# A transformer block on one core: the gated-shift copies rebuilt in one tensor, and the query/key weights loaded by head halves

## The chip, the cores and the metric

The kernel runs on one core of one Trainium2 chip. The metric is the device time of one execution in microseconds. Ten runs of the kernel before stand beside one profiled execution.

## The reference, cut to what matters

One sequence of 2048 rows with 448 features goes through attention over 8 dilated keys (16 heads of 28), and then through an MLP block whose first half shifts quarters of its features along the sequence:

```python
def _A_ref(x, wqkv, wo):                 # attention
    q, k, v = split(x @ wqkv)            # 16 heads of 28
    idx = pos[:, None] - 2 * arange(8)   # keys at 0, 2, ... 14 rows back
    attn = softmax(where(idx >= 0, q . k[idx] * scale, -1e9))
    return (attn . v[idx]) @ wo

def _B_ref(x, w1, w2, w3, w4):
    h = _gelu(_layernorm(x) @ w1)
    c = D // 4                           # 112
    g0 = h[:, :, 0*c:1*c] moved down one row      (zero row in front)
    g1 = h[:, :, 1*c:2*c] moved up one row        (zero row at the end)
    g2 = h[:, :, 2*c:3*c] moved down two rows
    g3 = h[:, :, 3*c:   ] moved up two rows
    hs = concatenate([g0, g1, g2, g3]) @ w2
    x1 = x + hs
    return x1 + _gelu(_layernorm(x1) @ w3) @ w4

h = x + _A_ref(_layernorm(x), wqkv, wo)
return h + _B_ref(_layernorm(h), w1, w2, w3, w4)
```

## The kernel before, in words

The sequence is cut into four chunks of 512 rows (c = 0 to 3). Inside a chunk, even and odd rows are kept apart as two parities p, so a shift by two rows is a shift by one column, and a shift by one row swaps the parities. All tensors are bf16 with sums in f32.

For each chunk the kernel normalises the rows and transposes them (phase_A1, L623; chunks 0 and 1 on TensorE, chunks 2 and 3 by transposing DMAs), projects values (phase_V, L654) and queries and keys (phase_QK, L700), forms scores, exponentials and weighted values (phase_att, L716: operations S, E and AV), divides by the sums (through a DMA to memory and back for chunks 2 and 3), projects with wo (phase_WO, L804), and enters the MLP: normalise and transpose by DMA, matmul with w1, gelu (phase_B1, L816). The second matmul with w2 (phase_B2, L877) and the large pair w3 and w4 (phase_W3, L900, phase_B3, L934) run over groups of tiles that lag the chunks (GROUPS, L871), since the shifts reach into the next chunk.

*Names.* Operations carry tags: V_c, QK_c.0 and QK_c.2 with evictions QK_c.e0 to e3, S_c.g, E_c.g, AV_c.g for head half g, WO_c, W1_c, W2_g, W3_g, W4_g. A PE operation V, QK, WO, W1, W2 or W3 is four passes of 64-row tiles that use both halves of the array at once (quad, L414); S uses 28-row tiles, AV 32-column tiles, W4 and the PE transposes the whole array.

*Order.* Nothing is scheduled at run time. Each operation is recorded once with its dependencies, and the table _ORDER (L235) writes out one global order by operation number, with a letter where the engine was open ("a" ACT, "v" DVE, "p" GpSimd) and the PSUM banks after the colon; schedule (L159) reads it, and _emit_plan (L194) adds the semaphore waits that the order doesn't already imply. Each engine then runs its part in order. All instructions are issued by one line (L1407), so the profile's line is the same everywhere and groups are told apart by tensor names. SP issues almost all DMAs; a DMA that has to wait for its data holds up those behind it on SP. START (L232; used at L1394 to L1400) sets at which instruction offset modulo 256 an engine's code starts. WARM (L229, L478) is the number of matmuls on zeros that TensorE runs while the first loads are under way.

*Loads at the start.* The four tiles of chunk 0 come first (L459, L460), on SP and ACT in turn; then wqk in two pieces of 448 KB and wv in two of 224 KB on SP (win_load, L449; each piece holds two of four row windows k of the weights); then chunks 1 to 3 of x. Query and key weights are then padded from 28 to 32 columns a head by four copies, one for each row window w (pad_wqk, L646 to L652), on ACT and DVE. QK needs all four.

*The shifted gelu.* W1_c yields two PSUM tiles. The first becomes gA with one gelu (L838). The second, three planes of 256 columns, becomes gtm with one gelu (L842). Then twelve copies put it, shifted, into gB (four copies of 32 rows and two planes, L844 to L847) and gC (eight of 32 or 16 rows and one plane, L848 to L852), each with its own offset for each group of rows; in the last chunk three DVE memsets clear edge columns (L853, L854). Each copy is on ACT or DVE, as _ORDER says (shift, L370). g_rows (L856) gives the matmul W2 its rows of gA, gB and gC. w1_p holds w1 with its columns permuted to match (L528 to L534), and w2_s its rows (L519 to L526).

## Time and profile before

| | us |
|---|---|
| median of 10 runs | 192.98 |
| lowest, highest | 192.15, 194.65 |
| profiled execution, its own time | 192.86 |
| its span | 191.1 |
| PE busy | 182.9 |
| DVE busy | 128.8 |
| ACT busy | 112.2 |
| GpSimd (POOL) busy | 41.8 |

The span runs from the first to the last instruction of the profiled execution; 1.76 us of its time lie around it. Busy times are sums over instructions; PE is matmul time, and loading of weights (PEld) lies beside it. In the timeline a row gives start, length, engine, operation, output and input tensor, their shape and a count; in brackets is the idle time before it and what ended it. "issue" there means that the engine waited for nothing that the profile shows. A name such as arena is shared: it holds the attention weights first and the large gelu later. w_p is w1_p, w_s is w2_s or a weight of the large pair, ps is PSUM.

### The profile page before, as it was taken

Reading aid. Unit: us, or ns where it says so; the run is one execution under the profiler, and the core shown is the slowest. Engines: PE = TensorE matmul, PEld = TensorE weight load, DVE = VectorE, ACT = ScalarE, POOL = GpSimd, SP = SyncE. Lnnn points to the kernel's source line nnn. Section 1 sums busy time; section 2 is a strip of 40 time slices with the busy share of each in tenths; the row PEclk is TensorE's granted clock in tenths of the full one; section 3 lists DMA queues with packets and bytes.
Section 4 is the critical chain, followed back from the end, with each engine's and each line's share of the span. In section 5 each row is a group of like instructions: output and inputs, shape, how many; then the busy total and the mean of one; then the engine's idle time right before and its main releaser. Section 6 shows DMA issues by size and latency. Waiting matters only on the chain.

```text
span 191.1 us, 6790 instructions
## 1 busy us (share of the span) xinstructions
PE 182.9 (96%) x2999; PEld 102.6 (54%) x2999; DVE 128.8 (67%) x313; ACT 112.2 (59%) x149; POOL 41.8 (22%) x101
## 2 busy tenths in 40 slices
PE   7899999998897998999999999999999999999994
PEld 2455556554555573577556464444566568454551
DVE  7799998999985789999773379894038970001241
ACT  2869899598859849938658930117691326554000
POOL 4137500607104503006900002043000320000000
PEclk9999999999999999999999999999999999999999
DMA  5965317325499765620641800507000233000021
GB/s 145 342 212 158 83 32 145 37 33 109 135 141 227 199 166 130 78 81 3 121 109 55 199 3 1 139 20 173 10 0 27 47 97 100 3 0 3 3 99 51
DMA packets 32479, 17.77 MB, mean 93 GB/s; under 512 B 22524, under 2 KB 31932, under 8 KB 32444
## 3 DMA queue, kind: packets, MB, share of 16 engines
q1 hardware_dynamic: 32156, 17.05, 38.5%
q8 instruction: 25, 0.41, 0.9%
q10 hardware_dynamic: 288, 0.23, 0.4%
q14 instruction: 10, 0.08, 0.1%
HBM read 10.07 MB, written 1.90 MB: 63 GB/s over the span
## 4 chain that ended last, share of the span: by engine, by line
PE 73%; ACT 10%; DVE 10%; DMA 4%; issue 1%
PE ps L1407 73%; DMA actT<-lntm 3%; ACT qk L1407 2%; ACT pt L1407 2%; DVE st L1407 2%; ACT gC L1407 2%; DVE rzb L1407 2%; DMA xin<-in_A_x_dram 1%; DVE osb L1407 1%; DVE xin L1407 1%; DVE oT L1407 1%; ACT gtm L1407 1%; ACT lntm L1407 1%; ACT arena L1407 1%; DVE lntm L1407 1%
## 5 line engine op out<-in xcount | busy, mean ns | idle before, releaser
L1407 PE MATMUL ps<-actT,w_s 64*128 64x512 bf16 (+2 forms) x560 | 44.2, 312 | 0.0
L1407 PE MATMUL ps<-w_s,arena 128*128 128x448 bf16 x224 | 43.4, 353 | 0.1
L1407 DVE TENSOR_TENSOR xb<-ps,xb 128x448 bf16<-128x448 f32 (+1 forms) x26 | 18.4, 724 | 32.8 <-PE ps L1407 32.7
L1407 ACT ACTIVATE arena<-ps 128x512 bf16<-128x512 f32 (+2 forms) x40 | 29.0, 767 | 16.9 <-PE ps L1407 16.6
L1407 PEld LDWEIGHTS ps<-actT,w_s 64*128 64x128 bf16 x560 | 26.4, 94 | 16.9 <-DVE xb L1407 0.4
L1407 PEld LDWEIGHTS ps<-w_s,arena 128*128 128x128 bf16 x224 | 21.4, 98 | 20.9 <-issue 0.6
L1407 PE MATMUL ps<-hT,arena 64*128 64x512 bf16 x224 | 25.9, 377 | 0.2
L1407 POOL TENSOR_TENSOR rstd<-vtmp,mhalf 128x4 f32<-128x4 f32 (+1 forms) x16 | 18.5, 1154 | 1.1
L1407 DVE BATCH_NORM_STATS2 st<-xin 128x6 f32<-128x448 bf16 x32 | 18.1, 606 | 0.1
L1407 ACT ACTIVATE pt<-ps 128x1024 bf16<-128x1024 f32 x16 | 15.7, 1022 | 3.3 <-PE ps L1407 3.2
L1407 PEld LDWEIGHTS ps<-hT,arena 64*128 64x128 bf16 x224 | 10.7, 94 | 12.0 <-ACT qk L1407 0.7
L1407 ACT ACTIVATE lntm<-xin,nmr,rstd 128x512 bf16<-128x512 bf16 x13 | 10.2, 808 | 9.0 <-POOL nmr L1407 8.5
L1407 POOL TENSOR_SCALAR vtmp<-mv 128x4 f32<-128x4 f32 (+1 forms) x16 | 4.6, 287 | 49.9 <-DVE mv L1407 49.0
L1407 PE MATMUL ps<-arena,hT 64*64 64x448 bf16 (+1 forms) x248 | 15.1, 352 | 0.3 <-DVE hT L1407 0.3
L1407 ACT ACTIVATE qk<-ps 128x1024 bf16<-128x1024 f32 x14 | 13.9, 1021 | 2.3 <-PE ps L1407 2.2
L1407 PE MATMUL ps<-wo_s,oT 64*128 64x448 bf16 x128 | 13.1, 350 | 0.6 <-ACT vt L1407 0.5
L1407 PE MATMUL ps<-actT,w_p 64*128 64x512 bf16 (+1 forms) x140 | 13.0, 333 | 0.2 <-DMA actT<-lntm 0.2
L1407 POOL TENSOR_SCALAR nmr<-mv 128x4 f32<-128x4 f32 (+1 forms) x16 | 3.9, 246 | 42.0 <-DVE mv L1407 41.8
L1407 ACT ACTIVATE lntm<-xb,nmr,rstd 128x512 bf16<-128x512 bf16 x5 | 4.0, 811 | 15.1 <-POOL nmr L1407 15.1
L1407 DVE COPY gC<-gtm 32x256 bf16<-32x256 bf16 (+1 forms) x15 | 3.4, 227 | 13.3 <-ACT gtm L1407 12.9
L1407 DVE TENSOR_TENSOR pt<-pt,msk 128x1024 bf16<-128x1024 bf16 x16 | 10.5, 682 | 0.6 <-ACT pt L1407 0.5
L1407 PEld LDWEIGHTS ps<-arena,hT 64*64 64x64 bf16 (+1 forms) x248 | 7.6, 107 | 5.7 <-DVE hT L1407 0.5
(90 smaller groups left out, 226.9 us busy)
## 6 DMA issues: line engine op xcount, KB each, us to landing
w_s<-in_B_w_dram SPq DMA_DIRECT2D x6, 448.0 KB, 4.9
rzb<-rz_scratch SPq DMA_DIRECT2D x8, 256.0 KB, 4.4
out_dram<-xb SPq DMA_DIRECT2D x16, 112.0 KB, 2.1
xin<-in_A_x_dram SPq DMA_DIRECT2D x3, 448.0 KB, 7.3
arena<-in_A_wqkv_dram SPq DMA_DIRECT2D x2, 448.0 KB, 5.8
w_s<-in_B_w_dram SPq DMA_DIRECT2D x2, 336.0 KB, 4.8
arena<-in_A_wqkv_dram SPq DMA_DIRECT2D x2, 224.0 KB, 5.1
w_s<-in_B_w_dram SPq DMA_DIRECT2D x2, 224.0 KB, 2.8
```

The source lines that it names most:

```text
L1407: inst = getattr(eng, meth)(**kw)
```

## The change

1. gB, gC and gtm become one tensor gBC with four planes. The second gelu writes planes 0 to 2 of the chunk's columns directly. Seven copies then work inside gBC: two move 32 rows of planes 0 and 1 left by one or two columns, one copies plane 2 of all 128 rows to plane 3, and four write shifted pieces of plane 2 over parts of plane 3, after that one. In the last chunk some of them are one or two columns longer, and the three memsets are gone. Edge clears and g_rows follow.
2. Columns of w1_p and the 16-row pieces of w2_s are permuted to match; their number is the same.
3. wv is loaded ahead of wqk in the program, and wqk comes in eight pieces of 128 x 2 x 224 elements (448-byte rows): by head half h, window pair k, and query or key e; pieces with e above h are on ACT's queue. The four pad copies go by (h, k), so that QK_0.0 needs two of them, and QK_0.2 the other two.
4. Costs that the order was planned with change (bw, occ, lat); these are not instructions.
5. WARM is 13 instead of 14, START 132 instead of 128, and _ORDER is written anew: 843 operations instead of 861. It moves work on every engine. The largest moves: the clear of wo_s and the masks' clears stand before the first statistics on DVE; the first exp table load follows the first transposed copies on ACT; both evictions QK_3.e2 and QK_3.e3 are on DVE; AV_2.0 and AV_2.1 both stand before W1_0; S_3.0 stands before W2_1 and W3_0 after WO_2; on SP the last transposing DMA of chunk 3 stands after the transposing DMA of chunk 0's MLP input and a load of w4; GpSimd's w1_p copies come later. PE issues 2998 matmuls instead of 2999, and changes its kind of tiling 48 times instead of 51.

```diff
@@ -226,47 +226,46 @@
         op.clock = oc
     return plan
 
-WARM = 14
+WARM = 13
 LATE = 2
 
-START = 128
+START = 132 
 _ORDER = """
-2 1 4 3 7 6 8 5 12 17 0 16 13 15 45 65 74 64 67 68 79 21 19 18:7 22 20 28 23 24 25 26 29 27 35 30 32 36:7 33:6
...
+18 2 71 80 0 23 21 20 22 85 84 19 70 88 73 24:7 1 3 8 68 69 4 65 11 10 9 27 74 25 28 32 26 29 34 30 33 35 36 31
...
 """.split() 
@@ -304,9 +303,7 @@
     zz = oT[:, 0, :]
     rzb = sb("rzb", [128, 4, 512], F32)
     gA = sb("gA", [128, 2, 2, HALF + 2], BF16)
-    gB = sb("gB", [128, 2, HALF + 4], BF16)
-    gC = sb("gC", [128, HALF + 4], BF16)
-    gtm = sb("gtm", [128, 2, 768], BF16)
+    gBC = sb("gBC", [128, 4, HALF + 4], BF16)
     xin = sb("xin", [128, NTL, D], BF16)
     xb = sb("xb", [128, NTL, D], BF16)
     lntm = sb("lntm", [128, 3, 4, 2, 256], BF16)
@@ -376,6 +373,8 @@
         if not on_pool:
             del op.opts["pool"]
         op.occ = {e: v - {"dve": 82, "pool": 20, "act": 93}[e] for e, v in op.lat.items()}
+        if not on_pool:
+            op.occ = {e: v + {"dve": 0, "act": 25, "pool": 0}[e] for e, v in op.lat.items()}
         return op
 
     def pool(meth, lat, **kw):
@@ -446,20 +445,26 @@
     def xt(t, c, il, n):
         return t[:, 4 * c:4 * c + 4, :].rearrange("p (a u) d -> p a u d", a=2) if n == 4 else t[:, 4 * c + il, :]
 
-    def win_load(name, dst, src, nbytes, engs):
+    def win_load(name, dst, src, nbytes, engs, bw=290.0):
 
         for k in range(2):
             dma("%s%d" % (name, k), dst[:, 2 * k:2 * k + 2, :],
                 src[192 * k:192 * k + 256, :].rearrange("(c k) n -> k c n", k=128), nbytes / 2, engs[k],
-                430.0)
+                430.0, bw)
 
     tag("init0")
     dve("memset", 320, ap=zz[:], constant=0.0)
     tag("load0")
     for il in range(4):
-        dma("x0_%d" % il, xt(xin, 0, il, 1), x_rows(A_x, 0, il, 1), 128 * D * 2, ("sp", "act")[il % 2])
-    win_load("wqk", wqk_s, A_wqkv[:, 0:2 * D], 512 * 2 * D * 2, ("sp", "sp"))
-    win_load("wv", wv_s, A_wqkv[:, 2 * D:3 * D], 512 * D * 2, ("sp", "sp"))
+        dma("x0_%d" % il, xt(xin, 0, il, 1), x_rows(A_x, 0, il, 1), 128 * D * 2, ("sp", "act")[il % 2], bw=450.0)
+    win_load("wv", wv_s, A_wqkv[:, 2 * D:3 * D], 512 * D * 2, ("sp", "sp"), 190.0)
+    for h in range(2):
+        for k in range(2):
+            for e in range(2):
+                o = D * e + D // 2 * h
+                dma("wqk%d%d%d" % (h, k, e), wqk_s[:, 2 * k:2 * k + 2, o:o + D // 2],
+                    A_wqkv[192 * k:192 * k + 256, o:o + D // 2].rearrange("(c k) n -> k c n", k=128), 128 * D * 2,
+                    "act" if e > h else "sp", 430.0, 280.0)
     tag("load1")
     for c in range(1, NCH):
         dma("x%d" % c, xt(xin, c, 0, 4), x_rows(A_x, c, 0, 4), 128 * 4 * D * 2)
@@ -506,9 +511,8 @@
         dve("memset", 480, ap=w1_p[:, :, 384:640], constant=0.0)
         pool("memset", 140, ap=gA[:, :, :, 0:1], constant=0.0)
         pool("memset", 140, ap=gA[:, :, :, HALF + 1:HALF + 2], constant=0.0)
-        pool("memset", 140, ap=gB[:, :, 0:2], constant=0.0)
-        pool("memset", 140, ap=gB[:, :, HALF:HALF + 2], constant=0.0)
-        pool("memset", 140, ap=gC[:, 0:2], constant=0.0)
+        pool("memset", 140, ap=gBC[:, :, 0:2], constant=0.0)
+        pool("memset", 140, ap=gBC[:, :, HALF + 2:HALF + 4], constant=0.0)
 
     def load_attn_out():
         tag("load2")
@@ -522,15 +526,14 @@
             128 * D * 2)
         for g in range(4):
             for h in range(2):
-                k = 64 * h + 32 * (g // 2) + 16 * (1 - g % 2)
+                k = ((32, 0, 48, 16), (64, 112, 80, 96))[h][g]
                 dma("w2%d" % (3 + 2 * g + h), w2_s[k:k + 16, 3, :], w2v[96:112, g, :], 16 * D * 2)
         w1v = w1_s[:].rearrange("k w (g d) -> k w g d", d=G)
         tag("w1p")
         shift(w1_p[:, :, 0:256].rearrange("k w (g d) -> k w g d", d=64), w1v[:, :, :, 0:64], 1024, True)
         shift(w1_p[:, :, 256:384].rearrange("k w (g d) -> k w g d", d=32), w1v[:, :, :, 64:96], 512, True)
         for x in range(2):
-            for g, o in ((x, 384), (2 + x, 480), (2 + x, 544), (x, 576)):
-                o += 16 * (1 - x)
+            for g, o in (((0, 416), (2, 464), (2, 560), (0, 576)), ((1, 384), (3, 480), (3, 528), (1, 624)))[x]:
                 shift(w1_p[:, :, o:o + 16], w1v[:, :, g, 96:112], 64, True)
 
     def load_mlp():
@@ -581,7 +584,7 @@
         op = S.add_many("flex", [("tensor_scalar", dict(kv, x=n_))], 0, 0)
         op.opts = {"dve": [("tensor_scalar", kv)],
                    "act": [("activation", dict(out=out_ap, in_=in_ap, func=ACT.Identity, scale=r_, bias=n_))]}
-        op.occ = {"dve": 308, "act": 652}; op.lat = {"dve": 390, "act": 745}
+        op.occ = {"dve": 310, "act": 710}; op.lat = {"dve": 390, "act": 805}
         return op
 
     def lslot():
@@ -648,8 +651,11 @@
         dve("memset", 230, ap=wv_2[:], constant=0.0)
         copy(wv_2[64:128, :], wv_s[64:128, 2, :], D, psum=False, mode=3.0)
         tag("pad")
-        for w in range(4):
-            copy(wqk_p[:, w, :, 0:28], wqk_s[:, w, :].rearrange("p (j d) -> p j d", d=28), 896, psum=False, mode=3.0)
+        for h in range(2):
+            for k in range(2):
+                copy(wqk_p[:, 2 * k:2 * k + 2, :, 0:28].rearrange("p w (e j) d -> p (w e) j d", e=2)[:, :, 8 * h:8 * h + 8, :],
+                     wqk_s[:, 2 * k:2 * k + 2, :].rearrange("p w (e j d) -> p (w e) j d", e=2, d=28)[:, :, 8 * h:8 * h + 8, :],
+                     896, psum=False, mode=3.0)
 
     def phase_V(c):
 
@@ -838,20 +844,17 @@
         act(gA[:, :, :, 1 + 256 * c:257 + 256 * c], T1(lambda p: p[:].rearrange("k u (p n) -> k u p n", p=2)),
             ACT.Gelu_apprx_tanh, 1024)
         tag("W1_%d.e1" % c)
-        gt = gtm[:, c % 2, :]
-        act(gt, T2(lambda p: p.rearrange("k u n -> k (u n)")[:, 0:768]), ACT.Gelu_apprx_tanh, 768)
+        o = 2 + 256 * c
+        act(gBC[:, 0:3, o:o + 256], T2(lambda p: p.rearrange("k u n -> k (u n)")[:, 0:768].rearrange("k (t n) -> k t n", t=3)),
+            ACT.Gelu_apprx_tanh, 768)
         tag("G_%d" % c)
-        for q, sh in enumerate((0, -1, 0, -2)):
-            r = slice(32 * q, 32 * q + 32)
-            o = 2 + 256 * c + sh
-            shift(gB[r, :, o:o + 256], gt[r, 0:512].rearrange("k (p n) -> k p n", p=2), 512)
-        for q, (s1, s2) in enumerate(((-1, 0), (-1, 1), (0, 1), (-1, 1))):
-            for m, sh in ((32, s2), (16, s1)):
-                r = slice(32 * q, 32 * q + m)
-                o = 1 + 256 * c + sh
-                shift(gC[r, o:o + 256], gt[r, 512:768], 256)
-                if c == NCH - 1 and m == 32 and s1 < 0:
-                    dve("memset", 145, ap=gC[32 * q:32 * q + 16, HALF:HALF + 1], constant=0.0)
+        last = c == NCH - 1
+        for r0, m, d, e in ((32, 32, 1, 1), (96, 32, 2, 2)):
+            v = gBC[r0:r0 + m, 0:2, :]
+            shift(v[:, :, o - d:o - d + 256 + e * last], v[:, :, o:o + 256 + e * last], 512)
+        for r0, m, d, e in ((0, 128, 0, 0), (0, 32, 2, 1), (32, 16, 1, 0), (96, 32, 1, 0), (96, 16, 2, 1)):
+            v = gBC[r0:r0 + m, :, :]
+            shift(v[:, 3, o - d:o - d + 256 + e * last], v[:, 2, o:o + 256 + e * last], 256)
 
     def g_rows(r, t, c, il):
 
@@ -865,8 +868,8 @@
             return gA[r, 1, p, n + o:n + o + 128]
         if t == 2:
             q, o = (p, 1) if hi else (1 - p, 1 if p == 0 else 2)
-            return gB[r, q, n + o:n + o + 128]
-        return gC[r, n + 1:n + 129]
+            return gBC[r, q, n + o:n + o + 128]
+        return gBC[r, 3, n + 1:n + 129]
 
     GROUPS = [[(0, 0), (0, 2)]] + [[(c, 1), (c, 3), (c + 1, 0), (c + 1, 2)] for c in range(3)] + [[(3, 1), (3, 3)]]
     pos = {}
```

## The prediction

> **What bounds the kernel now.** I read the page first: busy time by engine, the slices, the chain of waits.
>
> ```profile
> PE 182.9 (96%) x2999; PEld 102.6 (54%) x2999; DVE 128.8 (67%) x313; ACT 112.2 (59%) x149; POOL 41.8 (22%) x101
> ...
> PE   7899999998897998999999999999999999999994
> ...
> PE 73%; ACT 10%; DVE 10%; DMA 4%; issue 1%
> ```
>
> TensorE is busy 96% of the span at full clock, and its work hardly changes (2999 matmuls become 2998). So the change is worth the holes in PE that it closes, less those that it opens, and nothing else. The windows, stage by stage (length, PE, PEld, DVE, ACT, POOL busy, clock, DMA share, GB/s), say where holes are:
>
> ```profile
> 45.00:62.00 17.00, 15.01 (x435) 9.02 (x427) 14.30 (x29) 13.08 (x16) 4.93 (x10) 1.00 0.87 161
> 62.00:77.00 15.00, 14.47 (x189) 8.13 (x185) 12.44 (x33) 11.22 (x19) 4.37 (x11) 1.00 0.66 161
> ...
> 90.00:140.00 50.00, 50.00 (x589) 26.71 (x589) 29.35 (x73) 26.20 (x31) 10.89 (x19) 1.00 0.35 80
> 140.00:145.00 5.00, 4.68 (x52) 2.89 (x49) 2.84 (x12) 4.11 (x8) 0.00 (x0) 1.00 0.02 3
> ```
>
> From 90 to 140 there is nothing to win: 50.00 of 50.00. Holes lie before 90 and once at 144. The timeline names those that the change can touch:
>
> ```profile
> 3.50 1.15 DVE L1407 BATCH_NORM_STATS2 st<-xin 128x6 f32<-128x448 bf16 x2
> ...
> 8.47 1.33 PE L1407 MATMUL ps<-arena,hT 64*64 64x448 bf16 x24 [0.33 <-DVE hT L1407]
> 9.46 0.63 DVE L1407 COPY arena<-arena 128x896 bf16<-128x896 bf16 x1 [0.83 <-DMA arena<-in_A_wqkv_dram]
> ...
> 56.44 3.21 PE L1407 MATMUL ps<-actT,w_p 64*128 64x512 bf16 x35 [0.16 <-DMA actT<-lntm]
> 61.17 0.21 PE L1407 MATMUL ps<-pt,vt 64*32 64x51 bf16 x5 [0.83 <-issue]
> ...
> 73.11 2.18 ACT L1407 ACTIVATE gC<-gtm 32x256 bf16<-32x256 bf16 x5
> 75.32 1.02 ACT L1407 ACTIVATE qk<-ps 128x1024 bf16<-128x1024 f32 x1
> 76.39 0.55 PE L1407 MATMUL ps<-w_s,gA 64*128 64x448 bf16 x4 [0.53 <-ACT qk L1407]
> ...
> 140.47 0.81 ACT L1407 ACTIVATE gtm<-ps 128x768 bf16<-128x768 f32 x1
> 141.31 0.62 ACT L1407 ACTIVATE gB<-gtm 32x512 bf16<-32x512 bf16 x1
> 141.96 1.73 ACT L1407 ACTIVATE gC<-gtm 16x256 bf16<-16x256 bf16 x4
> 143.84 0.37 PE L1407 MATMUL ps<-w_s,gA 64*128 64x224 bf16 x4 [0.32 <-ACT gC L1407]
> ```
>
> At 76.39 PE waits for a query/key eviction that sat on ACT behind five shift copies; at 143.84 for the last shift copy itself; at 8.47 for the first transposed activations; around 61 for an instruction-side stall and then the activations of the last chunk. Prices of the copies, by tile:
>
> ```profile
> L1407 ACT ACTIVATE gC<-gtm x17: 412/414/419, 60.8 to 143.3; 16x256 bf16<-16x256 bf16 x11, 32x256 bf16<-32x256 bf16 x6
> L1407 DVE COPY gC<-gtm x15: 215/221/299, 64.3 to 143.2; 32x256 bf16<-32x256 bf16 x10, 16x256 bf16<-16x256 bf16 x5
> ...
> L1407 DVE COPY gB<-gtm x13: 217/285/291, 63.7 to 142.8; 32x512 bf16<-32x512 bf16 x13
> L1407 ACT ACTIVATE gB<-gtm x3: 625/626/634, 63.0 to 141.3; 32x512 bf16<-32x512 bf16 x3
> ```
>
> **What the Trainium skill says.** "DMA: Bandwidth & Descriptors", Specifications, puts 512 B as the smallest transfer at line rate; the change cuts the query/key rows to 448 B. The trace before has packets of 256 B at 18 ns, 896 B at 41 and 1792 B at 74, and none of 448. The same page, "Issuing engines are not separate DMA queues": moving loads to ACT's queue gives issue time only, not bandwidth. "Runtime: NRT & Kernel Launch", Instruction fetch mechanics: code arrives in blocks of 256 instructions, and crossings are mostly hidden. The trace agrees but for two: PE stops inside an operation at 45.83 (0.36 us) and 61.17 (0.83 us) with "issue" as the releaser, both times at its 256th instruction boundary. "ScalarE: Activation LUTs", What ACT_TABLE_LOAD costs, gives 1283 ns; the seven loads here take 1.28 us each.
>
> **The change part by part** (start of a PE operation after, less before).
>
> *Start.* Three memsets move ahead of the first statistics, the 0.81 us clear of wo_s among them, while one of 0.2 moves back: DVE's clears end 0.6 later, so statistics start at 4.08, not 3.50. TensorE's warm-up matmuls, one fewer, start as much later and end near 6.7, still ahead of the first transposes (7.2), so they cost nothing. And the order of the normalisations, transposes and evictions behind is closer (PE took two batches of transposes with 0.55 and 0.27 us waits): walking each with its duration gives the first V matmul at 8.75, +0.28. The best is 0 (load-bound chain unaffected), the worst is the wv load, below.
>
> *Loads by halves.* The same 1.38 MB lie ahead of the last wv piece. A 448-B packet costs about 25 ns on the line through 256 and 896 B, at most 41 (the 896-B price: half the rate). At 25 wv lands 0.4 later, under 8.75, hidden by the normalisations; at 41 it lands 1.0 to 1.4 later, some 9.6 to 9.9, and V waits: 0 to +1.1. I take 0, because 448 B lies between two measured prices. The gain is that the first QK needs pads of half the heads only: two DVE copies of 0.65 after the load, done near 11.0 while QK starts near 11.5, so both are hidden by V (2.9 us); without that cover DVE's 0.83 us wait at 9.46 would show. Eight issues take the place of two, six more at 0.4 us on SP or ACT; they stand behind x0, and delay x1 to x3, first read after 15, nothing.
>
> *First softmax.* The exp table load (1.28 us, on the chain at 15.79) moves to about 9, under V. PE then reaches the second score group without its 0.4 us hole, but at 20.6 against 20.58, because the +0.28 and more ACT work before it eat that. Net +0.02.
>
> *20 to 52.* No step is removed. The new order has other evictions late by some 0.3 (second QK group of chunk 2: +0.28). GpSimd's w1 copies move to about 31 to 35, off PE's path. WO_1, which waited 0.7 us for oT, starts at 52.0 against 52.35: −0.35, of which 3 fewer changes of tiling at 0.09 (by the matmul starts) are a part that comes by 62.
>
> *52 to 62.* W1_0 needs the transpose issued at 52.05, 3.7 to 5.3 us long in the trace, so 55.8 to 57.3; AV_2.0 and AV_2.1 now both stand ahead of it and cover it to 57.1. The last transpose for QK_3 is issued behind tr2 and a w4 load at about 55.2 on SP; such took 3.6 to 5.5, so QK_3 starts between 59.2 and 60.8. I take 60.4. Before, this point, with the extra AV half (0.77) taken off, is 60.75: −0.35 (−1.4 to +0.1). The START change moves boundaries in PE's code, not the stall at 45 (same matmul), so I keep 0.4 there; the 0.83 at 61.17 now falls elsewhere, and I price it at 0.4, half.
>
> *Shift copies.* Seven copies for twelve. On ACT in chunk 1 there are still five (128x256, 32x512 and three of 256: 0.41+0.63+3x0.41 = 2.3 us against 2.18), so ACT gets no relief; but QK_3.e3 goes to DVE, whose work in this chunk falls from 7 copies to 2 (about 1.8 to 0.5), which pays for the second 1.23 us eviction. PE's 0.7 us hole at 76 shrinks to 0.15: −0.55. Copies wait now for one another across ACT and DVE, since they rewrite plane 3: in chunk 1 DVE's copy waits for ACT's 128-row one (0.41), with QK_3.e2 behind it; in chunk 3 ACT's third copy waits for DVE's 128-row one, which starts with the gelu and takes 0.22, while ACT does a 0.63 one first. Both waits are covered; uncovered they would cost 0.2 each. In chunk 3 ACT falls from 0.62+1.73 to 0.63+0.41+0.41 = 1.45 after the gelu, and DVE from about 2.1 to 1.0. With all earlier by the 1.0 gained before, the gelu ends at 140.3, the last copy at 141.7, and PE arrives at 142.5: W2_4 loses its 0.5 us step but for a switch of tiling, −0.4 (0 to −0.5). In chunks 0 and 2 the copies end well ahead of W2; nothing.
>
> *77 to 90.* WO_2 waits for a softmax that now has the table load ahead of it, +0.1; at 88 to 90 the gelu wait before W4_0 is shorter, −0.2.
>
> Sum: at QK_3 −0.35, then −0.55 +0.1 −0.2 −0.4 = −1.4. Span 191.1 − 1.4 = 189.7; the profiled execution took 192.86, 1.76 around its span, hence 191.5. The median of the runs is 0.12 above that execution: 191.6.
>
> **The rivals.**
> (A) *Slower: the last transpose of chunk 3.* It is moved behind tr2 and a w4 load on SP's queue. For QK_3 after the point 60.75, each us costs a us, and the other terms give 1.05: landing at 61.8 uses up all, and from 62.8 on the kernel is slower by over 0.5%. That is 7.6 us after issue. For it: DMA is busy 0.87 of this window, and w4's own load took 5.8 us before. Against it: 5.5 is the most that any transpose took. At 63.0 the time is 192.98 + 2.25 − 1.05 = 194.2.
> (B) *wv late at the start.* 448-B rows at 41 ns: V at 9.9, +1.1, which the slack behind does not take up: 191.6 + 0.9 = 192.5, no change.
> (C) *It is off the path.* ACT and DVE get shorter, but PE was waiting for their other work: holes at 76 and 144 stay or are found again at the next wait: 192.4 to 193.2.
> (D) *More.* Transpose at 59.2 and no fetch stall: 190.5.
>
> **How the numbers follow.** A measurement of this kernel tells about 0.5%, 0.96 us. Forecast 191.6 (191.0 to 192.0), 0.44; D 0.18; B 0.10; C 0.12; A 0.16. Faster: forecast and D, 0.62. Same: B and most of C, 0.20. Slower: A, and 0.02 of C with new holes, 0.18. The range, 190.3 to 193.9, takes in D, B and C and leaves out A.
>
> **What would show it.** First bn_stats at 4.1 and V at 8.5 to 9.0 (wv late: V near 9.9, waiting for DMA). QK_3.0 before 61. No hole over 0.3 at W2_1 and W2_4, and the ACT copies of the last chunk gone by 142. ACT's five copies in chunk 1 near 2.3 us. 90 to 140 still without a hole. The forecast is wrong if new holes of over 0.5 us come between 20 and 52, where 50 DVE and 28 ACT instructions change place and I only walked the order.

## The result, and the profile after

| | before | after |
|---|---|---|
| median, us | 192.75 (51 runs) | 194.14 (14 runs) |
| lowest, highest, us | 192.12, 194.65 | 193.38, 197.06 |
| profiled execution, its own time | 192.86 | 195.94 |
| its span | 191.1 | 194.2 |

After stands at 1.0078 of before, with an interval of 1.0059 to 1.0097: slower by 0.8%, where 191.6 (0.6% faster) was forecast. The profiled execution of after lies 1.8 us above its own median, so its trace holds more than the median shows; which of its holes are common to all executions has to be asked of other runs. In some executions, the profiled ones of e1, e2, e4, f7 and g2 below among them, the TensorE clock was below full in one stretch and the time 1 to 5 us longer, so the time at full clock stands beside the median where it matters, and of such a profile the rest is read.

The page of after, busy time, slices and chain:

```profile
PE 182.1 (94%) x2998; PEld 102.7 (53%) x2998; DVE 123.0 (63%) x288; ACT 113.5 (58%) x150; POOL 37.8 (19%) x101
...
PE   6699979998997899999998999999999999999994
...
PE 80%; ACT 7%; DVE 5%; issue 3%; DMA 2%; POOL 2%; ACTq 0%
```

TensorE's busy time fell by 0.8 us and DVE's by 5.8, the latter as fewer shift copies let one expect, but the span grew by 3.1. "issue" rose from 1% to 3% of the chain. Two stages of before that the prediction does not show, and then the stages of after, with the columns as there:

```profile
0.00:20.00 20.00, 18.03 (x244) 9.02 (x245) 17.59 (x52) 13.82 (x18) 8.86 (x30) 1.00 0.67 205
20.00:45.00 25.00, 24.58 (x818) 13.63 (x815) 23.76 (x54) 21.34 (x29) 7.37 (x20) 1.00 0.36 68
```

```profile
0.00:20.00 20.00, 16.59 (x231) 8.25 (x233) 16.63 (x51) 12.81 (x17) 8.59 (x30) 1.00 0.76 198
20.00:45.00 25.00, 23.39 (x762) 13.23 (x760) 22.19 (x48) 19.78 (x29) 5.68 (x17) 1.00 0.30 62
45.00:62.00 17.00, 15.61 (x469) 8.91 (x468) 15.48 (x32) 13.95 (x17) 4.41 (x11) 1.00 0.87 154
62.00:77.00 15.00, 13.15 (x178) 8.05 (x180) 8.47 (x24) 11.63 (x16) 4.41 (x12) 1.00 0.59 135
77.00:90.00 13.00, 12.69 (x234) 7.81 (x232) 12.46 (x22) 8.53 (x13) 0.28 (x2) 1.00 0.41 121
90.00:140.00 50.00, 49.26 (x661) 26.87 (x657) 30.66 (x74) 26.52 (x34) 11.49 (x24) 1.00 0.37 76
140.00:145.00 5.00, 5.00 (x66) 3.67 (x63) 0.20 (x1) 4.31 (x7) 0.00 (x0) 1.00 0.06 17
```

PE is busy for less time than before up to 20 (16.59 us against 18.03), from 20 to 45 and from 62 to 77. From 45 to 62 it is busy for more, though it still stands for 1.4; since after runs late, a stage no longer holds the same work. From 90 to 140 there is a new loss of 0.74 us, where before had none, and from 140 to 145 the hole is gone. The timeline gives each hole a name:

```profile
2.78 0.81 DVE L1410 MEMSET wo_s<- 128x896 uint32 x1
...
4.04 1.09 DVE L1410 BATCH_NORM_STATS2 st<-xin 128x6 f32<-128x448 bf16 x2
...
9.37 2.84 PE L1410 MATMUL ps<-arena,hT 64*64 64x448 bf16 x56 [0.22 <-issue]
...
26.93 0.69 PE L1410 MATMUL ps<-pt,vt 64*32 64x51 bf16 x66 [1.41 <-issue]
...
48.26 0.22 PE L1410 MATMUL ps<-qk 28*64 28x51 bf16 x5 [0.60 <-issue]
...
59.38 2.56 PE L1410 MATMUL ps<-actT,w_p 64*128 64x512 bf16 x26 [0.21 <-DMA actT<-lntm]
63.85 1.90 PE L1410 MATMUL ps<-hT,arena 64*128 64x512 bf16 x16 [1.91 <-ACT gA L1410]
...
79.78 0.55 PE L1410 MATMUL ps<-w_s,gA 64*128 64x448 bf16 x4 [0.17 <-DVE qk L1410]
...
103.14 3.21 PE L1410 MATMUL ps<-actT,w_p 64*128 64x512 bf16 x34 [0.58 <-issue]
...
146.93 0.37 PE L1410 MATMUL ps<-w_s,gA 64*128 64x224 bf16 x4
```

V_0 starts at 9.37 (8.47 before). PE stops inside AV_0.1 for 1.41 and inside S_2.1 for 0.60. QK_3.0 waits 1.91, the largest hole. W2_1, at 79.78, waits 0.17 (0.53 before), and W2_4, at 146.93, not at all (0.32 before). W1_2 waits 0.58.

Starts of the same PE operations, us from the span's start, with two experiments that are told below:

| | before | after | e3_tr32_first | f1_memset_late |
|---|---|---|---|---|
| V_0 | 8.47 | 9.37 | 9.08 | 8.40 |
| V_2 | 48.24 | 50.68 | 49.71 | 48.36 |
| V_3 | 64.64 | 67.63 | 64.62 | 63.40 |
| WO_2 | 80.15 | 82.74 | 79.74 | 78.51 |
| AV_3.0 | 95.11 | 97.90 | 94.89 | 93.67 |
| W1_2 | 99.67 | 103.14 | 100.17 | 98.92 |
| last matmul | 187.94 | 191.02 | 188.05 | 186.80 |

**The wait at QK_3.0.** The profile names ACT's gelu into gA, which ended at 63.66. SP's queue tells another story. The rows are start, length of the issue, and what was issued, first of after:

```profile
54.44 3.14 SPq L1410 DMA_TRANSPOSE actT<-lntm  x1
57.63 0.59 SPq L1410 DMA_DIRECT2D w_s<-in_B_w_dram  x1
58.26 1.20 SPq L1410 DMA_TRANSPOSE hT<-lntm  x1
```

These are tr2 (for the MLP input of chunk 0), the weight load w40 (448 KB) and tr3_2, the last transposing DMA of chunk 3. Of tr3_2 the view by tile (hT, from 57.2 to 59) says:

```profile
L1410 SPq DMA_TRANSPOSE hT<-lntm x1: 1200/1200/1200, 58.3 to 58.3; - x1
DMA to landing us min/median/max: 5.5/5.5/5.5
```

58.26 + 5.5 = 63.76, and QK_3.0 starts 0.09 later. It is the transpose. The same place of SP's queue in before, with the landing of the two transposes into hT, at 52.7 and 55.7:

```profile
51.08 1.60 SPq L1407 DMA_TRANSPOSE actT<-lntm  x1
52.72 2.34 SPq L1407 DMA_TRANSPOSE hT<-lntm  x1
55.11 0.58 SPq L1407 DMA_DIRECT2D w_s<-in_B_w_dram  x1
55.73 1.20 SPq L1407 DMA_TRANSPOSE hT<-lntm  x1
...
DMA to landing us min/median/max: 4.1/4.8/5.5
```

In before, too, a 448 KB weight load (w310, a piece of w3) stands right ahead of the last transpose (there tr3_0), which landed after 5.5 at 61.23, while PE came at 61.52. So point 5 of the change, which has the last transpose moved behind tr2 and a weight load, names no real move: it stood behind both already, and counted from the start of V_2 it is issued 7.49 us off in before and 7.58 in after, and lands 12.99 and 13.08 off. What changed is PE. It runs out of work 11.26 after V_2 (at 61.94) instead of 13.28. Of these 2.02 us, 1.19 are in the AV operations (0.83 of it the stop in AV_2.0 that before has), 0.58 are the last pass of W1_0, which now stands behind QK_3.0, and 0.25 are WO_1's shorter wait.

### The profile page after: what moved, and what is told of

Read it like the earlier page. It is cut to its first block, busy times and chain, and to the rows that moved or that the text cites. A ratio compares the mean times of both kernels' runs of the same rounds, so it can differ in the third digit from the quotient of the medians.

```text
span 194.2 us, 6763 instructions
## 1 busy us (share of the span) xinstructions
PE 182.1 (94%) x2998; PEld 102.7 (53%) x2998; DVE 123.0 (63%) x288; ACT 113.5 (58%) x150; POOL 37.8 (19%) x101
## 4 chain that ended last, share of the span: by engine, by line
PE 80%; ACT 7%; DVE 5%; issue 3%; DMA 2%; POOL 2%; ACTq 0%
PE ps L1410 80%; DVE st L1410 2%; DMA xin<-in_A_x_dram 2%; ACT pt L1410 1%; ACT qk L1410 1%; DVE xin L1410 1%; ACT vt L1410 1%; ACT L1410 1%; ACT osb L1410 1%; POOL vtmp L1410 1%; DVE xb L1410 1%; POOL rstd L1410 1%; ACT gA L1410 1%; DVE mv L1410 1%; ACTq L1410 0%
## 5 line engine op out<-in xcount | busy, mean ns | idle before, releaser
L1410 PE MATMUL ps<-actT,w_s 64*128 64x256 bf16 (+2 forms) x560 | 44.3, 312 | 0.0
L1410 POOL TENSOR_SCALAR vtmp<-mv 128x4 f32<-128x4 f32 (+1 forms) x16 | 5.3, 334 | 94.6 <-DVE mv L1410 94.0
L1410 ACT ACTIVATE lntm<-xin,nmr,rstd 128x512 bf16<-128x512 bf16 x16 | 12.6, 812 | 8.3 <-POOL nmr L1410 8.2
L1410 POOL TENSOR_TENSOR rstd<-vtmp,mhalf 128x4 f32<-128x4 f32 (+1 forms) x16 | 16.3, 1021 | 0.9
L1410 ACT ACTIVATE qk<-ps 128x1024 bf16<-128x1024 f32 x12 | 12.0, 1024 | 3.8 <-PE ps L1410 3.7
L1410 DVE COPY gBC<-gBC 32x256 bf16<-32x256 bf16 (+5 forms) x15 | 3.6, 246 | 16.0 <-ACT gBC L1410 15.6
L1410 ACT ACTIVATE lntm<-xb,nmr,rstd 128x512 bf16<-128x512 bf16 x6 | 4.7, 810 | 13.9 <-POOL nmr L1410 13.9
L1410 PEld LDWEIGHTS ps<-actT,w_p 64*128 64x128 bf16 x140 | 8.4, 94 | 4.9 <-issue 1.0
```

The source lines that it names most:

```text
L1410: inst = getattr(eng, meth)(**kw)
```

## The experiments

Each edit is against the kernel named. Numbers in the order are operations. Ratios are to the kernel before on the same chip. An operation "stops" where PE stands still in the middle of it with "issue" as the releaser.

**What made after slow: four runs.** Theory T: tr3_2 behind w40. Rivals: x0_3 behind a weight load on ACT's queue (the start), and the stop in AV_0.1.

e1_x0_first (after, with wqk001, number 8, behind the last tile of x, number 4):

```diff
-24:7 1 3 8 68 69 4 65
+24:7 1 3 68 69 4 8 65
```

> The changed kernel with one edit: on ACT's queue the last tile of chunk 0 (x0_3) is issued ahead of the first query/key piece (wqk001) instead of behind it. Theory: in the changed kernel that tile landed at 5.92 instead of 3.99, and this alone made the first V matmul late (9.37 against 8.47, where 8.75 was forecast). Then it lands near 4.1, V starts at 8.5 to 8.8, and the time falls by about 0.6 us (the 0.62 by which the second score group was late), ratio to the kernel before near 1.004. Rival (the loads' bytes as such, or the memsets moved ahead on DVE, make the start late): V stays past 9.2 and the time does not move.

Measured: 195.33, 1.0113 [1.0090, 1.0137] (6 runs). x0_3 landed at 4.20 instead of 5.92, yet V_0 started at 9.11. So x0_3 alone is not what holds V, and this theory of the start falls. Why the kernel is slower than after (195.23 at full clock) I can't say. QK_3.0 still waits 2.06, although this trace has no stop in AV_0.1.

e2_av01_late (after, AV_0.1 put back behind QK_1.2, PSUM banks renamed to suit):

```diff
-235 244:54 175a 201a 174 245 246 247 248 236 249 196 199a 237 232 250 113
+235 175a 201a 174 236 196 199a 237 232 113
...
-203 179 180 176a 110
+203 179 180 244:54 245 246 247 248 249 250 176a 110
```

> The changed kernel with AV_0.1 put back behind the four passes of QK_1.2, as the kernel before has it, with its normalising steps and the PSUM banks that this needs (banks of V_1.4, S_1.0, V_1, WO_0, S_1.1 and V_2.4 renamed). Theory: AV_0.1 close behind AV_0.0 makes TensorE run through a block of 256 instructions in 3.6 us, faster than the next one was fetched (5.15 us in that trace), and PE stood 1.6 us inside AV_0.1; with QK_1.2 between, the interval is some 5 us or more and the stop is gone: V_1.4 starts 1.2 to 1.6 earlier, time lower by 1.0 to 1.6 (ratio 0.999 to 1.002). Rival (the stop was chance of the one profiled execution, or its time is given back at the next wait for ACT or DVE): the time moves by less than 0.4.

Measured: 197.48, 1.0223 [1.0188, 1.0258]; 196.5 (1.9% over before) at full clock. The stop is gone, but two new waits take its place: 0.47 for a query/key eviction at 26.42, and 1.90 at V_1, for an eviction of attention sums into osb (34.01). The edit can't give the stop's price: it moves more than the stop.

e3_tr32_first (after, w40, number 133, behind tr3_2):

```diff
-275 532 133 276 277 526
+275 532 276 277 526
...
-525 280a 221 420 419 421
+525 280a 221 133 420 419 421
```

> The changed kernel with the last transposing DMA of chunk 3 (tr3_2) issued ahead of the 448 KB load w40 on SP, instead of behind it. Theory: the load's bytes stand in the same rings, so the transpose landed at 63.76 only, 5.5 us after issue and just after the load (63.20), and QK_3.0 waited 2.1 us. Ahead of the load it lands 3 to 4 us after its issue, near 61.5 or earlier, and QK_3.0 waits 0 to 0.4: time lower by 1.2 to 2.0 (ratio 0.997 to 1.001). Rival (transposes take 5 us in this window whatever stands ahead of them): lands at 62.5 or later, time lower by 0 to 0.8.

Measured: 192.94, 1.0015 [0.9993, 1.0037]: 0.6% under after. SP's queue and PE in e3:

```profile
53.48 2.90 SPq L1408 DMA_TRANSPOSE actT<-lntm  x1
56.42 1.27 SPq L1408 DMA_TRANSPOSE hT<-lntm  x1
57.73 0.58 SPq L1408 DMA_DIRECT2D w_s<-in_B_w_dram  x1
...
DMA to landing us min/median/max: 4.3/4.3/4.3
...
58.47 2.56 PE L1408 MATMUL ps<-actT,w_p 64*128 64x512 bf16 x26
60.84 1.92 PE L1408 MATMUL ps<-hT,arena 64*128 64x512 bf16 x16
61.84 1.03 ACT L1408 ACTIVATE gA<-ps 128x1024 bf16<-128x1024 f32 x1
```

tr3_2 took 4.3 from issue to landing instead of 5.5, and landed 11.03 after V_2 instead of 13.08: 1.2 us because it took less time, 0.87 because it was issued earlier. QK_3.0 starts without a wait, and from V_2 to V_3 the trace is 2.0 us shorter than that of after (the medians differ by 1.2). It starts a full us ahead of the gA gelu of this run (61.84), so QK_3.0 never needed that gelu: the releaser that the profile named in after is wrong. Theory T holds.

e4_all_three (after with the three edits above together):

> The three edits of the changed kernel together (x0_3 first on ACT's queue, AV_0.1 behind QK_1.2, tr3_2 ahead of w40). Theory that the three holes are what makes the changed kernel slower, and the rest of the forecast holds: time lower than the changed kernel's by 2.3 to 3.5 us, 190.8 to 191.9, ratio to the kernel before 0.990 to 0.996. Rival (the new order of engines gives it back elsewhere, as at W1_2 where PE waited 0.7 us for a DMA): ratio 0.997 to 1.003.

Measured: 196.28, 1.0155 [1.0125, 1.0185]; two executions at full clock took 194.95 and 195.2, 1.1% over before. It has what e3 gives, for QK_3.0 doesn't wait here, but also e2's new waits (0.47, and 1.86 at V_1). I missed the expected 190.8 to 191.9 by putting three edits into one kernel before each was known.

**The same edit from another kernel.** h3b_tr20_only is after with tr2_0 (number 196, the first transposing DMA of chunk 2) later in the order, which moved its issue little. h2b_tr32_tr20 is the same with e3's edit on top. The edit of h3b:

```diff
-249 196 199a 237
+249 199a 237
...
-208 349 350 202 198
+208 349 350 196 202 198
```

> The changed kernel with tr2_0 moved right ahead of tr2_3 and nothing else. Theory: the stop in AV_0.1 is gone, the wait of 2 us at QK_3.0 stays; as the stop came in about half of the runs, the median falls by 0.4 to 1.0 (ratio 1.003 to 1.006) and the spread of the runs shrinks. Rival: the wait at QK_3.0 takes it all back, since the transposing DMA for it is late whenever it is issued (ratio 1.0078 as it is).

> The changed kernel with two moves on SP alone: tr3_2 ahead of w40, and tr2_0 right ahead of tr2_3. Theory: both DMA places together are why the changed kernel is slower and not faster: ratio to the kernel before 0.996 to 1.000 (e3, with tr3_2 alone, had 1.0015, and some of its runs lay 1.2 us above the others). Rival: as e3.

Measured: h3b 194.19, 1.0066 [1.0049, 1.0083]; h2b 192.75, 0.9990 [0.9964, 1.0015]. tr3_2 landed 5.3 us after issue behind w40 and 2.5 ahead of it; QK_3.0 started 12.26 and 10.94 after V_2. With e3 that is two pairs for 0.6 to 0.8%, and the place of one DMA issue is all that differs in each.

**The start.** f1_memset_late is e3 with wqk001 behind x0_3 as in e1, and the clear of wo_s (84) behind the pads of QK_0.0:

```diff
-20 22 85 84 19 70 88
+20 22 85 19 70 88
...
-12 53v 54v 50 141
+12 53v 54v 84 50 141
```

> The changed kernel with tr3_2 ahead of w40 (as e3), and two edits at the start: the 0.81 us clear of wo_s stands behind the pad copies of QK_0.0 on DVE again, and x0_3 is ahead of wqk001 on ACT's queue. Theory: the clear ahead of the first statistics is what makes the first V matmul 0.6 late (with x0_3 early alone, V stayed at 9.1): statistics start at 3.5 or earlier, V at 8.3 to 8.6, and the time is lower than that of e3 by 0.3 to 0.6. Rival: the loads set the start (wv's last piece landed at 7.8 to 8.3), V stays at 9, time unchanged; or the gain is given back before the second score group, as ACT's work there is the limit.

Measured: 192.24, 0.9975 [0.9956, 0.9995]. DVE and PE in f1:

```profile
3.61 1.15 DVE L1408 BATCH_NORM_STATS2 st<-xin 128x6 f32<-128x448 bf16 x2 [0.43 <-DMA xin<-in_A_x_dram]
...
8.40 2.84 PE L1408 MATMUL ps<-arena,hT 64*64 64x448 bf16 x56 [0.18 <-issue]
```

The first statistics start at 3.61 here, where DVE even waits for x, and at 4.04 in after. V_0 comes 0.68 earlier than in e3 (9.08), and every start of the table moves by that or more. Since e1 shows that x0_3 alone moves V little (9.11), it is the clear that costs, alone or together with x0_3; the clear late with x0_3 late was not run.

f5_wqk_two_loads (e3, wqk in two loads of 448 KB again; the order renumbered):

```diff
-    for h in range(2):
-        for k in range(2):
-            for e in range(2):
-                o = D * e + D // 2 * h
-                dma("wqk%d%d%d" % (h, k, e), wqk_s[:, 2 * k:2 * k + 2, o:o + D // 2],
...
+    win_load("wqk", wqk_s, A_wqkv[:, 0:2 * D], 512 * 2 * D * 2, ("sp", "sp"))
```

> The changed kernel with tr3_2 ahead of w40 (as e3), and the query/key weights loaded in two pieces of 448 KB on SP in the order of the kernel before (wv0, wqk1, wv1, wqk0), so without the 448-byte rows; pads and everything else stay. Theory: the halves bring nothing to the end of the chain, since QK_0.0 waits for V, not for its weights: QK_0.0 starts within 0.2 of 11.86 and the time within 0.3 of e3. Rival one (448-byte rows slow the start): V and all after it 0.3 to 0.6 earlier. Rival two (halves are needed now that QK_0.0 has only two pads ahead of it): wqk0 lands at 9.4, pads end near 10.5, nothing is lost; if it lands after 10.5, QK_0.0 is late by as much.

Measured: 192.54, 0.9982 [0.9965, 0.9998]. V_0 starts at 8.87 against 9.08, and QK_0.0 at 11.65 against 11.86. g1_two_loads_memset_late (f5 with the clear late):

> The changed kernel with tr3_2 ahead of w40, the query/key weights in two loads (as f5) and the clear of wo_s behind the pads of QK_0.0 (as f1). Theory: halves of the loads cost 0.2 us or more at the start and gain nothing, the early clear costs 0.6, and both add up: V starts at 8.2 to 8.4, ratio to the kernel before 0.993 to 0.997. Rival: with V at 8.4 the weights become the limit, as wqk0 lands at 9.4 and the pads of QK_0.0 end at 10.6 only, so that the ratio is that of f1 (0.9975) or above.

Measured: 193.71, 1.0016 [0.9997, 1.0035]. V_0 comes at 8.68, after a wait of 0.47, where f1 with its halves has it at 8.40. Neither difference at V_0 (0.21 and 0.28) is larger than what kernels with the same start show among themselves (9.08 to 9.37, and 8.39 to 8.65), and the medians go opposite ways: f5 is 0.3% under e3, g1 0.4% over f1. So no gain or loss of the halves is resolved. Their 448-B packets took 25 ns each, as estimated.

**The shift copies.** f3_twelve_copies is e3 with each of the five copies of one plane done twice, the second into memory that nothing reads; its number of copies is again twelve:

```diff
-    def shift(out_ap, in_ap, n, on_pool=False):
+    def shift(out_ap, in_ap, n, on_pool=False, twice=None):
...
+        if twice is not None:
+            for calls in op.opts.values():
+                calls.append((calls[0][0], dict(calls[0][1], out=twice)))
```

> The changed kernel with tr3_2 ahead of w40 (as e3), in which each of the five one-plane shift copies is done twice, the second time into a dead part of w1_s: twelve copies a chunk again, in the same places of ACT and DVE, 0.41 us more on ACT and 0.22 on DVE for each. Theory (the forecast's): the smaller number of copies, with the eviction moved off ACT, is what took away the holes of 0.7 at W2_1 and 0.5 at W2_4; with twelve they come back in part: ACT's five copies in chunk 1 take 4.0 instead of 2.4, time higher than e3 by 0.4 to 1.2. Rival (off the path: the eviction moved to DVE did it, the number of copies does nothing): time within 0.3 of e3.

Measured: 193.48, 1.0066 [1.0043, 1.0089], 0.5% over e3. W2_1 in e3, and then in f3 with the copies on ACT that precede it:

```profile
76.78 0.55 PE L1408 MATMUL ps<-w_s,gA 64*128 64x448 bf16 x4 [0.17 <-DVE qk L1408]
```

```profile
72.48 0.42 ACT L1416 ACTIVATE gBC<-gBC 128x256 bf16<-128x256 bf16 x1
72.81 0.40 ACT L1416 ACTIVATE w_s<-gBC 128x256 bf16<-128x256 bf16 x1
...
75.56 0.40 ACT L1416 ACTIVATE w_s<-gBC 32x256 bf16<-32x256 bf16 x1
75.86 0.52 ACT L1416 ACTIVATE vt<-ps 128x448 bf16<-128x448 f32 x1
76.40 1.28 ACT L1416 ACT_TABLE_LOAD   x1
...
76.53 0.56 PE L1416 MATMUL ps<-w_s,gA 64*128 64x448 bf16 x4 [0.46 <-ACT vt L1416]
```

With the copies doubled, ACT's eviction into vt is late and PE waits 0.46 for it, nearly the 0.53 of before, and 0.34 instead of 0.14 at WO_2 behind the delayed exponentials. So fewer copies do pay: about 1 us ± 0.6. At W2_4, though, only 0.07 us of the 0.32 of before came back, so most of that gain is not shown to come of the number of copies.

**Stops inside an operation.** f7_start_4 is e3 with START 4, which only moves PE's code against its boundaries:

```diff
-START = 132
+START = 4
```

> The changed kernel with tr3_2 ahead of w40 (as e3), with START 4 instead of 132: not an instruction of TensorE's program is changed, only the places where its 256-instruction boundaries fall. Theory: the stops inside S_2.1 (0.8 to 1.1 us here, 1.6 in AV_0.1 in the changed kernel's trace) come where two boundaries follow one another sooner than a block is fetched, some 3.6 us at the least. With START 4 the boundaries fall so that five intervals would be 1.2 to 2.8 us by e3-like times: stops inside AV_0.0, AV_0.1, QK_2.2, AV_2.1 and AV_3.1 of together 6 to 10 us, and S_2.1's goes: time higher by 5 to 9. Rival (the stops have another cause, such as semaphores or PSUM): time within 1 of e3, stop still at the 75th matmul of S_2.1.

Measured: 203.33, 1.0474 [1.0416, 1.0532]. Three of its four executions had the clock below full; the fourth took 200.56, 4.0% over before and 7.6 us over e3, within what was expected. PE in f7:

```profile
27.68 0.51 PE L1408 MATMUL ps<-pt,vt 64*32 64x51 bf16 x44 [1.00 <-issue]
...
65.42 0.41 PE L1408 MATMUL ps<-pt,vt 64*32 64x52 bf16 x33 [1.67 <-issue]
...
107.40 0.24 PE L1408 MATMUL ps<-pt,vt 64*32 64x51 bf16 x12 [2.85 <-issue]
```

All the AV operations together idle 7.7 us in f7 and 0.1 in e3, and nothing but the boundaries has moved; the stop in S_2.1 of e3 (0.84) is gone in exchange. That the stops belong to the boundaries can also be counted. Every stop of over 0.3 us inside an operation stands at the same remainder of PE's instruction count modulo 256: 128 in the kernels with START 132, 0 in f7, and 132 in before and g3, which have START 128.

g2_s21_later (f1, the second pass of QK_2.0, number 384, ahead of S_2.1) and g3_before_s21_later (the same move in before) try to take the stop in S_2.1 away by a wider interval:

```diff
-270 273a 134 530:04 223
+270 273a 134 384 530:04 223
```

> As f1, with the second pass of QK_2.0 moved ahead of S_2.1, so that the boundary at the 75th matmul of S_2.1 comes 0.87 us of work later. Theory (TensorE there runs ahead of its instructions): the interval from the boundary in AV_1.1 grows from 3.1 to 3.9 or 4.0 us, the stop of 0.8 to 1.0 shrinks to 0 to 0.2, the exponentials of S_2.1 come no later than before, and the time falls by 0.5 to 0.9 (ratio 0.993 to 0.996). Rival (the stop is tied to S_2.1 itself, or only moves to the next wait, WO_1 or QK_3.0): time within 0.3 of f1.

> The kernel before, with only the second pass of QK_2.0 moved ahead of S_2.1, as in g2. Theory: its stop inside S_2.1 (step 0.54) is the same stop, so 0.3 to 0.6 are gained up to V_2; but QK_3.0 waits there for a transposing DMA that landed at 61.27 and for the stop in AV_2.0, which take it back unless they come earlier too: time lower by 0 to 0.5. Rival: no change at S_2.1.

Measured: g2 193.08, 0.9991 [0.9972, 1.0010]; g3 193.09, 1.0008 [0.9995, 1.0021]. The stop shrank below what the timeline marks in g2 and stayed at 0.35 in g3, but in both V_2 then waits 0.68 for the exponentials of E_2.1, which S_2.1 feeds later. The hole moved to the next wait.

h1b_tr20_later (f1) and i1_tr20_behind (f1) move tr2_0, whose packets lie beside the code's in the 20s. h1b puts it right ahead of tr2_3 (number 202), as h3b does, and i1 behind it. The edit of i1:

```diff
-208 349 350 202 198
+208 349 350 202 196 198
```

> As f1 (tr3_2 ahead of w40, x0_3 ahead of wqk001, the clear of wo_s late), with the first transposing DMA of chunk 2 (tr2_0) issued at about 26 us, right ahead of tr2_3, instead of at 21.4. Theory: the stop of 1.5 us in AV_0.1 comes when TensorE's instruction fetch, asked for at the boundary in S_0.1, finds the packets of tr2_0 ahead of it; with tr2_0 4 us later it never does: no stop in AV_0.1, the upper group of times (192.6 to 193.6) is gone, median 191.5 to 192.0, ratio 0.992 to 0.996. Rival (the stop comes of itself, the interval of 3.6 us being too short): the two groups stay.

> As f1, with tr2_0 behind tr2_3 on SP, so that it is issued at about 27.5 instead of 21.4. Theory: TensorE's fetch after the boundary in S_0.1 then finds no packets of a transpose ahead of it, starts 1.1 us after the boundary as it does elsewhere, and the stop in AV_0.1 is gone in the trace and in the runs: fast runs in one group, median 191.5 to 192.0, ratio 0.992 to 0.996. Rival (the stop comes of the short interval alone): stop of over 1 us in AV_0.1 in the trace, or two groups of times as in f1.

Measured: h1b 193.38, 1.0000 [0.9979, 1.0021]; i1 193.37, 1.0017 [0.9997, 1.0037]. h1b's edit did not move the issue (21.5 as in f1). i1's did, to 29.0, and the stop is still there, with another ahead of it:

```profile
21.63 0.24 PE L1408 MATMUL ps<-qk 28*64 28x51 bf16 x11 [0.68 <-issue]
...
26.40 0.69 PE L1408 MATMUL ps<-pt,vt 64*32 64x51 bf16 x66 [1.04 <-issue]
```

That tr2_0's packets cause the stop is refuted. The stop in AV_0.1 is in 9 of the 15 profiles with the changed order at that place and absent from 6, f1's among them. In the nine, the fetch of code behind S_0.1 began 3.2 to 3.9 us after the start of S_0.1, in the six 1.5 to 1.7; no run moved this on purpose. The times of f1 look like two groups: 13 of 19 executions lie at 191.5 to 192.4, the other 6 at 192.6 to 193.6. That these are the executions without and with the stop is likely but not shown, since the time of an execution doesn't tell where it stopped.

**The hole ahead of W1_2.** It needs tr0, a transposing DMA of chunk 0's second normalisation. g4_av31_later (f1, AV_3.1 and its eviction behind two passes of W3_1.00):

```diff
-344 668:2 669v 571 486 662a 487:40 488 489
+344 571 486 662a 487:40 488 668:2 669v 489
```

> As f1, with AV_3.1 moved behind two passes of W3_1.00. Theory: PE's wait of 0.75 at W1_2, seen in each trace of the changed order and not in the kernel before, comes from one of TensorE's instruction fetches: it is asked for at the boundary in AV_3.1, 1.4 to 1.5 us after the transposing DMA for W1_2 is issued (1.8 in the kernel before), runs between that DMA's packets, and the DMA's last part lands 1.0 us after the fetch has ended in every trace. With the boundary some 0.4 later the fetch falls behind the transpose, which then lands in 4.2 us or less instead of 5.9: the wait at W1_2 goes, time lower than f1 by 0.4 to 0.8. Rival (the DMA is slow by its place in the queue, ahead of the two small ones of zp): it lands 5.8 after issue as before, time within 0.3 of f1.

Measured: 192.96, 0.9983 [0.9961, 1.0006]. tr0 still landed 5.95 after issue. The wait at W1_2 shrank from 0.59 to 0.09, but one of 0.46 came ahead of W3_1.00, so nothing was gained. h4b_w31_before_av3 puts two W3_1.00 passes ahead of AV_3.0 and AV_3.1 in h1b (banks renamed), i2_tr20_w31 does it with i1's edit:

```diff
-343:4 661:6 344 668:2 669v
+343:4 487:20 488 661:6 344 668:4 669v
```

> As h1, with two passes of W3_1.00 moved ahead of AV_3.0 and AV_3.1 (and PSUM banks 2 and 4 exchanged from there on, so that they can be). Theory: TensorE's boundary in AV_3.1 comes 1.6 us later, its fetch starts after the transposing DMA for W1_2 has landed, which then takes under 4.5 us instead of 5.9, and the wait of 0.75 at W1_2 shrinks to 0.1 to 0.3 (the evictions of AV_3 come later and may be next): time lower than h1 by 0.3 to 0.7. Rival one: the DMA lands as late as before. Rival two: W3_1.00 now waits for its own transposes, which landed at 94.8 where it would start, and gives the gain back.

> As h4b (two passes of W3_1.00 ahead of AV_3), with tr2_0 behind tr2_3 as in i1. Theory: both meetings of a transposing DMA with an instruction fetch are avoided; h4b's two fastest runs were at 190.9 and 191.1, which would be those without the stop in AV_0.1: median 190.9 to 191.6, ratio 0.989 to 0.993. Rival: as h4b, 0.998.

Measured: h4b 192.82, 0.9980 [0.9961, 0.9999]; i2 193.15, 0.9990 [0.9969, 1.0010]. tr0 landed 4.27 and 4.28 after issue, and the time from the end of W4_0 to W1_2 fell by 0.46 and 0.47. W1_2 in before, h1b and h4b:

```profile
99.67 3.19 PE L1407 MATMUL ps<-actT,w_p 64*128 64x512 bf16 x35
```

```profile
100.56 3.21 PE L1408 MATMUL ps<-actT,w_p 64*128 64x512 bf16 x35 [0.64 <-issue]
```

```profile
100.11 3.21 PE L1408 MATMUL ps<-actT,w_p 64*128 64x512 bf16 x35
```

In the medians that is 0.2% ± 0.3, which these runs don't resolve. In after, the first part of tr0 landed at 101.35 and the last at 103.05; a block of PE's code was fetched from 101.06 to 102.03. In before the fetch ended (98.51) when tr0 had long landed (97.77). The last part came 1.03 us behind the end of that fetch in each trace in which tr0 took 5.9. So tr0 and a fetch run at the same time in the new order; that the fetch delays it is supported by the two moved kernels, not proved.

**Is there a version that beats both?** f1 has the lowest median, 192.24. That it beats after by 1.0% is clear (0.9975 against 1.0078). Whether it beats before stays open: h1b, whose edit left its DMA where f1 has it, came out at 1.0000, so that near-identical programs differ here by as much as f1's gain.

## Why the prediction was wrong, step by step

The failed step is "52 to 62". There the prediction let QK_3 start at 60.4, because its transpose "is issued behind tr2 and a w4 load at about 55.2". The transpose was issued at 58.26, took 5.5 us, which is the prediction's upper end, and landed at 63.76; QK_3.0 waited 1.91 for it and started at 63.85. So the mis-sized term is the time of the issue, 3.1 us too early:
- About 2.4 of it came from upstream, as V_2 itself was late: 0.9 at the start, 1.41 for the stop in AV_0.1, the rest in S_2.1.
- About 0.65 came on SP: the issues of tr2 and w40 took 3.82 us from 54.44 (tr2 alone 3.14, against 1.60 in before), where the forecast left 3.15 from 52.05.

The stop in AV_0.1, which not every execution has, does not explain it alone: e1's trace is without it, and there too tr3_2 was issued at 56.64 and landed at 62.44, so that QK_3.0 started at 62.53, 2.1 us after the forecast.

Behind this lies a misreading of before. The prediction took "the extra AV half (0.77)" off PE's time there, but both halves of AV_2 stand ahead of QK_3.0 in both kernels; what went behind it is W1_0's last pass. And it counted what PE gains without asking which landing PE's work had covered: in before the last transpose came only 0.3 us ahead of PE (61.23 against 61.52), so that nearly all that PE gained ahead of QK_3.0 became waiting. (Its range, "−1.4 to +0.1", is −1.55 to +0.05 by its own 59.2, 60.8 and 60.75.)

Rival A named the right wait. Its objection, "5.5 is the most that any transpose took", was true, but it was the issue that came late; the break-even point of 61.8 lies only 3.5 us behind the real issue. That its 194.2 comes so close to 194.14 is in part luck, since its sum has no loss at the start, no stop in AV_0.1 and no hole at W1_2. By the medians the late transpose is worth 1.2 us (after less e3). The other 1.3 of the 2.5 us between forecast and median is in e3 too, and comes from the terms below.

*Start.* "Statistics at 4.08": 4.04, right. "First V matmul at 8.75, +0.28": 9.37 in after, 9.08 in e3, so +0.6 to +0.9. The statistics' delay of 0.54 came through whole. The prediction gave 0.3 of it back for a closer order of the normalisations, and nothing came back: DVE is busy without a hole from 2.15 to about 8.2 in e3 and in after, so what is put ahead of its work makes it end later by as much. f1 gets it back.

*Loads by halves.* "25 ns" a packet: right, and rival B (wv late) did not happen. "They stand behind x0" was wrong: wqk001 stood ahead of x0_3 on ACT's queue and delayed it by 1.7 us, which by itself cost V nothing to speak of (e1).

*First softmax.* S_0.1 started at 21.20 (20.90 in e3, 20.22 in f1) against the forecast 20.6. That fits the start's loss.

*20 to 52.* "No step is removed", and holes of over 0.5 us here were named as what would make the forecast wrong. They came: the stop in AV_0.1, of 1.0 to 1.6 us in 9 of 15 profiles. The prediction kept 0.4 for S_2.1, where 0.53 to 0.93 was seen in the kernels that keep its place, and 0.4 for a stop somewhere else. Pricing the boundaries at a fixed 0.4 each was the second failed step. WO_1 lost half of its wait (0.51 to 0.27).

*Shift copies.* Right in kind. At W2_1 the hole went from 0.53 to 0.17 (forecast −0.55, seen −0.36), and W2_4's 0.32 is gone (forecast −0.4). f3 shows that the number of copies counts at W2_1, which makes rival C, "off the path", wrong there. At W2_4 the hole is gone as forecast, but f3 does not show that the number of copies did it.

*77 to 90.* WO_2 waits 0.14, against 0.07 in before (forecast +0.1). The −0.2 at W4_0 did not come: from WO_2 to W4_0 it is 9.57 us in before and 9.60 in e3.

*"From 90 to 140 there is nothing to win".* There was something to lose: 0.74, most of it ahead of W1_2, where tr0 lands late as a fetch of code runs beside it. The prediction put this stage at nothing because PE had no hole there in before.

The sum in e3, which has the change without the late transpose, as starts against before: +0.6 at V_0, +1.47 at V_2, −0.02 at V_3, −0.41 at WO_2, +0.50 at W1_2, +0.11 at the end. So e3 wins back 1.5 us between V_2 and V_3 and 0.4 at W2_1, and the start, the stops and W1_2 take it away again. Even of the 1.5, some is luck rather than design: 0.83 is before's stop in AV_2.0, which is gone because the boundaries fall elsewhere; 0.24 is WO_1's wait and 0.16 W1_0's.

What stays open: why the code's fetch behind S_0.1 begins late in some executions and not in others, what made tr2's issue hold SP twice as long as in before, and why e1 was slower than after.

## What to carry to other kernels

When an edit takes work from the engine that sets the end, look up which landing that work was covering, and how much slack it had. Here it was 0.3 us, and nearly all that PE gained ahead of QK_3.0 became waiting. Then walk the queue that issues this landing again, with the predecessors' issue times and with all that comes late upstream. Before moving a clear to the front, look whether the first matmul waits for the same engine's work behind it. And between two orders of the same instructions a few tenths of a per cent may be nothing but where the code's blocks begin: test that with an edit that only shifts the boundaries before explaining a small difference.

## What the runs showed of the hardware

The Trainium skill, "Runtime: NRT & Kernel Launch", Instruction fetch mechanics, calls crossings of an instruction block mostly hidden. The trace of before agrees but for two stops (0.36 and 0.83 us). That of f7 does not: there a shift of the boundaries alone made the kernel 4.0% slower than e3 in the one execution at full clock, with single stops of up to 2.85 us, most of them inside AV operations, whose matmuls follow one another every 9 ns (160 in 1.5 us). "DMA: Bandwidth & Descriptors", Specifications, names 512 B as the smallest transfer at line rate; here the 448-B packets took 25 ns, on the line between the 256-B and the 896-B ones (18 and 41 ns), with no step. The transposing DMA tr3_2 took 2.5 to 4.4 us from issue to landing ahead of the 448 KB load w40 on its queue, and 5.3 to 5.8 behind it. The issue of a transposing DMA held SP for anything from 1.2 us (tr3_2) to 3.1 us (tr2, both in after).
